# Half-width weight loads, longer filler bursts and a small fill moved from GpSimd to ScalarE, in an attention-and-mixer kernel on one Trainium2 core

## The chip, the cores and the metric

The kernel runs on one core of a Trainium2 chip. The metric is the device time of one execution in microseconds (us). "PE" is the matmul engine (TensorE), "PEld" its weight load, "ACT" ScalarE, "DVE" VectorE, "POOL" GpSimd, "SP" SyncE, which issues most of the DMAs. "L887" is line 887 of the kernel. The changed kernel is nine lines longer, so that L887 of the kernel before is L889 in the kernel after, L700 is L702, L453 is L454, L461 is L462 and L463 is L464.

## The reference

Two layers (the same weights twice), each an attention block and a token mixer. The sequence has S = 2048 tokens of D = 640 features; there are H = 32 heads of only 20 features each. A "chunk" below is a block of 128 x 512 scores, and the "crossing" is the way from the first layer to the second.

```python
def _A_ref(x, wqkv, wo):                       # attention
    qkv = (x @ wqkv).reshape(B, S, 3, H, Dh).transpose(2, 0, 3, 1, 4)
    q, k, v = qkv[0], qkv[1], qkv[2]
    p = _softmax(einsum("bhqd,bhkd->bhqk", q, k) * Dh ** -0.5)
    o = einsum("bhqk,bhkd->bhqd", p, v)
    return o.transpose(0, 2, 1, 3).reshape(B, S, D) @ wo
def _B_ref(x, w1, b1, w2, b2):                 # mixer over the tokens
    u = gelu(einsum("bsd,sf->bdf", layernorm(x), w1) + b1)
    return (einsum("bdf,fs->bds", u, w2) + b2).transpose(0, 2, 1)
x = A_x
for _ in range(2):                             # written out in the reference
    x = x + _A_ref(_layernorm(x), A_wqkv, A_wo)
    x = x + _B_ref(_layernorm(x), B_w1, B_b1, B_w2, B_b2)
```

One layer has 32 x 2048 x 2048 exponentials. They are the bulk of the work of ACT and DVE (L887 with 1520.2 of ACT's 1581.0 us busy, L840 and L860 with 507.4 and 636.4 of DVE's 1464.6, in the profile before); the score and P.V matmuls around them are the bulk of PE's (L700 and L927, with 575.2, 500.6 and 465.7 us, some of it at the same time, of 1646.1).

## The kernel before

The kernel is a Python program that plans its own order: a model of the engines (with constants such as `M_T`, `LAT_V`, `PAD_V`, `FILL_NS`) picks, one step at a time, what each engine does next, and emits the instruction. The order that comes out is fixed; each engine has its own list, with waits on semaphores where data are needed from another engine (section 1 shows a piece of ACT's list with its waits). Those waits are added by a tracker that compares which memory each instruction writes and reads.

The parts that matter here, with cuts marked `# ...`:

```python
PAD_V = 450.0
FILL_NS = 400.0                    # longest burst of filler matmuls, in ns of the model

# scores S: four 32-row tiles of the PE array side by side
pe(nc.tensor.matmul(dst, lhsT=k_, rhs=q_, start=True, stop=True, tile_position=(32 * j, 0)))      # L700
# their exponentials: most chunks by ACT ...
nc.scalar.activation(out=P[...], in_=St[...], func=ACT.Exp, scale=SCALE)                          # L887
# ... and some by DVE, with integer arithmetic (for a group of four chunks: L840 once for each chunk, then L860 five times)

# "filler" work of PE: projections, output projection, mixer, taken up between S and P.V
def do_fill(start, f, n):          # n is FILL_NS
    # ...
    while t - start < n:
        # ... stop before S would be late, or where the data are not there yet
        f["mms"][f["idx"]](f["tile"])
        t += f["cost"]
        # ...

# weights of Q (i = 1) and K (i = 0): one DMA into a staging tile, then five copies that spread
# the heads from 20 to 32 columns
def load_w(i):
    wr = sb("wraw", [128, NDT, D], BF16, i)
    # ...
    dma(wr[:], A_wqkv[:, coff:coff + D].rearrange("(dt p) n -> p dt n", p=128), 128 * NDT * D * 2,
        rate=DMA_RATE * (0.5 if i else 0.9), then=lambda t: pad_copies(i, wr, t))
def pad_copies(i, wr, t):
    wpad = wq_pad if i else wk_pad
    for dt_ in range(NDT):
        def f(s, eng, dt_=dt_):
            copy(eng, w_view(wpad, dt_)[:, :, 0:DH], wr[:, dt_, :].rearrange("p (h i) -> p h i", i=DH))
            # ...

# the constant columns of V: 20 values, then a one and three zeros, for each head and key tile
nc.scalar.activation(out=v_pad.bitcast(F32), in_=..., func=ACT.Copy, scale=0.0)
nc.scalar.activation(out=v_pad[:, :, 0:1], in_=..., func=ACT.Copy, scale=-2.0)                    # L1615
nc.gpsimd.memset(Vaug[:, NKT * H * VW:], 0.0)
nc.gpsimd.memset(Vv[:, :, H // 2, 0:32 - VW], 0.0)                                                # L1618
```

In the profile the staging tile appears as "JT" and the tile of V's weights as "attnT", because they share memory with those. `pst` is PSUM.

The softmax here doesn't subtract the row's maximum and nothing guards it: scores larger than these inputs give would overflow.

## Time and profile before

| | |
|---|---|
| time, first three runs | 1725.9 us, median of 3 (1723.1 to 1727.19) |
| time in the rounds of the kernel after (those three and one more) | 1726.55 us, median of 4 |
| time, in the five batches of experiments | 1724.36, 1724.84, 1724.95, 1724.72, 1724.65 us, medians of 9 to 11 |
| span of the profiled run, granted clock | 1722.5 us, 0.995 |

The page of the kernel before: first the busy time of each engine with its share of the span, then three groups of instructions (count, busy time and mean ns of one, idle time before them and its main releaser).

```profile
PE 1646.1 (96%) x21916; PEld 641.2 (37%) x21917; DVE 1464.6 (85%) x2630; ACT 1581.0 (92%) x1427; POOL 167.5 (10%) x261
...
L887 ACT ACTIVATE P<-pst 128x1536 bf16<-128x1536 f32 (+1 forms) x1335 | 1520.2, 1311 | 26.9 <-PE pst L700 14.5
L860 DVE TENSOR_SCALAR JT<-JT 128x2048 uint16<-128x2048 uint16 x950 | 636.4, 701 | 5.0 <-PE pst L927 1.8
L700 PE MATMUL pst<-QT,KT 32*128 32x512 bf16 (+1 forms) x4224 | 575.2, 377 | 40.7 <-ACT P L887 28.5
```

Busy time by stretches of the kernel before (start and end in us, length, then busy us of PE, PEld, DVE, ACT, POOL with their counts, the granted clock, the DMA share and GB/s).

```profile
0.00:20.00 20.00, 14.42 (x94) 6.23 (x98) 13.53 (x43) 12.45 (x16) 8.02 (x28) 0.83 0.67 221
20.00:40.00 20.00, 18.54 (x259) 7.16 (x253) 14.34 (x38) 19.45 (x20) 4.89 (x13) 1.00 0.12 35
...
100.00:400.00 300.00, 290.33 (x3580) 95.53 (x3580) 282.03 (x483) 294.78 (x262) 25.24 (x30) 1.00 0.03 8
...
780.00:1000.00 220.00, 210.17 (x3419) 110.81 (x3415) 118.70 (x248) 177.66 (x181) 22.36 (x49) 1.00 0.23 72
```

From 100 to 400 us ACT is busy 294.78 of 300 us and PE 290.33: these two engines leave little to win by a better order there. What is loose lies at the start and at the crossing between the layers (780 to 1000 us), where PE is full and ACT is not.

The timeline of the start, kernel before (start, length, engine, line, operation, count; in brackets the idle time just before it and what ended it):

```profile
7.84 0.20 POOL L1618 MEMSET Vaug<- 128x128 bf16 x1 [5.69 <-ACT Vaug L1615]
8.13 0.19 POOL L354 TENSOR_SCALAR rt<-mv 128x1 f32<-128x1 f32 x1
...
5.24 2.55 ACT L1615 ACTIVATE Vaug<-mhalf 128x512 bf16<-128x512 f32 x1
...
9.50 0.59 PE L541 MATMUL pst<-ident,attnT 128*128 128x128 bf16 x5 [3.30 <-DVE attnT L530]
...
13.71 3.03 PE L453 MATMUL pst<-hh,wq 128*128 128x512 bf16 x7 [0.24 <-DVE wq L463]
...
19.36 0.39 PE L700 MATMUL pst<-QT,KT 32*128 32x512 bf16 x3
```

POOL's tiny memset waits 5.69 us for ACT's fill of V's constant columns, and behind it in POOL's list stands the first step of the layernorm (`rt`), whose input was ready near 4.2 us. The way to the first score matmul at 19.36 us leads through it. PE is idle for 3.30 us before 9.50 us, and half clock follows (0.50 in the windows from 10 to 15 us). By the clock records of this trace it lasts 6.83 us, from 9.67 us on; the other windows of half clock within the span, in this trace, last 3.41 or 6.83 us. These records hold no granted clock but 1.00 and 0.50.

### The profile page before, as it was taken

What the parts mean: (1) busy time and instruction counts of PE and PEld (TensorE: products, weight loads), DVE (VectorE), ACT (ScalarE), POOL (GpSimd) and SP (SyncE); (2) the same over time, 40 slices, a digit from 0 to 9 for tenths busy, and PEclk for the clock granted to TensorE, in tenths of its full rate; (3) what the DMA queues carried; (4) which work ended last, traced back from release to release, by engine and by line L of the source; (5) the groups of instructions that cost most, each with busy time, mean ns of one, the idle gap of its engine ahead of it and who ended that gap; (6) DMA issues with size and microseconds to landing.
All of it is one profiled execution on the core that took longest, in us unless ns stands there. A gap on an engine that the chain in (4) does not pass through costs nothing. (4 is left out here: it accounts for less than half of the span.)

```text
span 1722.5 us, 50500 instructions
## 1 busy us (share of the span) xinstructions
PE 1646.1 (96%) x21916; PEld 641.2 (37%) x21917; DVE 1464.6 (85%) x2630; ACT 1581.0 (92%) x1427; POOL 167.5 (10%) x261
## 2 busy tenths in 40 slices
PE   8999999999999999998999999999999999998989
PEld 3433333332333333335545432333333333332356
DVE  6688999999989999999444489999999888999963
ACT  7899999999999999997598899999999999999950
POOL 3100002000200020001100000110011000200010
PEclk9999999999999999999999999999999999999999
DMA  3200001000112106511422000100002120257143
GB/s 119 29 2 2 2 13 36 2 1 2 52 57 71 39 32 190 182 34 43 148 84 75 25 2 2 33 32 1 1 17 58 57 70 32 76 179 216 42 125 95
DMA packets 103295, 98.06 MB, mean 57 GB/s; under 512 B 45600, under 2 KB 79520, under 8 KB 103072
## 3 DMA queue, kind: packets, MB, share of 16 engines
q1 hardware_dynamic: 99456, 94.82, 17.8%
q8 instruction: 171, 2.80, 0.7%
q0 software_dynamic: 3616, 0.01, 0.3%
q14 instruction: 52, 0.43, 0.1%
HBM read 63.35 MB, written 31.46 MB: 55 GB/s over the span
## 5 line engine op out<-in xcount | busy, mean ns | idle before, releaser
L887 ACT ACTIVATE P<-pst 128x1536 bf16<-128x1536 f32 (+1 forms) x1335 | 1520.2, 1311 | 26.9 <-PE pst L700 14.5
L860 DVE TENSOR_SCALAR JT<-JT 128x2048 uint16<-128x2048 uint16 x950 | 636.4, 701 | 5.0 <-PE pst L927 1.8
L700 PE MATMUL pst<-QT,KT 32*128 32x512 bf16 (+1 forms) x4224 | 575.2, 377 | 40.7 <-ACT P L887 28.5
L840 DVE TENSOR_SCALAR JT<-pst 128x512 uint16<-128x512 f32 x760 | 507.4, 679 | 63.9 <-PE pst L700 61.5
L927 PE MATMUL pst<-P,Vaug 128*32 128x512 bf16 (+1 forms) x3440 | 500.6, 380 | 3.4 <-DVE T_85 L977 1.8
L927 PE MATMUL pst<-JT,Vaug 128*32 128x512 bf16 (+1 forms) x3920 | 465.7, 380 | 3.4 <-DVE T_85 L977 2.4
L700 PEld LDWEIGHTS <-KT 32*128 32x128 bf16 x4224 | 168.5, 91 | 512.2 <-issue 498.5
L927 PEld LDWEIGHTS <-Vaug 128*32 128x32 bf16 x7360 | 170.2, 94 | 297.3 <-issue 268.0
L1002 POOL TENSOR_TENSOR T_86<-T_85,rden 128x512 bf16<-128x512 f32 x64 | 67.5, 1054 | 1130.6 <-DVE rden L989 1090.8
L1066 PE MATMUL pst<-wo,attnT 128*32 128x320 bf16 x2048 | 111.3, 301 | 4.7 <-DVE attnT L1012 3.2
L456 PEld LDWEIGHTS <-W 128*32 128x32 bf16 x3384 | 89.7, 96 | 60.0 <-issue 28.8
L1488 PE MATMUL pst<-ident,zw 128*32 128x512 bf16 (+1 forms) x330 | 108.8, 380 | 0.0
L456 PE MATMUL pst<-hh,wq 128*32 128x512 bf16 x1232 | 104.3, 382 | 1.3 <-DVE JT L840 0.7
L456 PE MATMUL pst<-hh,wk 128*32 128x512 bf16 x1240 | 97.3, 381 | 1.1 <-DVE JT L840 0.6
L456 PE MATMUL pst<-x1last,W 128*32 128x320 bf16 x1536 | 80.6, 301 | 0.9 <-DVE JT L840 0.5
L1066 PEld LDWEIGHTS <-attnT 128*32 128x32 bf16 x2048 | 52.4, 96 | 42.2 <-issue 20.3
L456 PE MATMUL pst<-attnT,hh 128*32 128x320 bf16 x1196 | 60.2, 300 | 2.1 <-DVE hh L463 0.7
L463 DVE CAST KT<-pst 128x512 bf16<-128x512 f32 x53 | 36.0, 680 | 19.5 <-PE pst L456 18.3
L456 PE MATMUL pst<-JT,W 128*32 128x320 bf16 x1080 | 52.3, 300 | 0.0
L977 DVE STREAM_TRANSPOSE T_85<-pst 128x512 f32<-128x512 f32 (+1 forms) x58 | 40.0, 690 | 8.1 <-PE pst L927 8.0
L354 POOL TENSOR_SCALAR rt<-mv 128x1 f32<-128x1 f32 x64 | 13.4, 209 | 340.2 <-DVE mv L346 339.6
L463 DVE CAST Vaug<-pst 128x320 bf16<-128x320 f32 x43 | 20.6, 482 | 30.4 <-PE pst L456 21.6
(91 smaller groups left out, 878.0 us busy)
## 6 DMA issues: line engine op xcount, KB each, us to landing
W<-in_B_w_dram SPq DMA_DIRECT2D x10, 768.0 KB
W<-in_B_w_dram SPq DMA_DIRECT2D x24, 256.0 KB
xs<-in_A_x_dram SPq DMA_DIRECT2D x32, 160.0 KB
x2d<-xs SPq DMA_DIRECT2D x16, 320.0 KB
xs<-x2d SPq DMA_DIRECT2D x16, 320.0 KB
x1d_69<-xs SPq DMA_DIRECT2D x12, 320.0 KB
uacca_72<-W SPq DMA_DIRECT2D x12, 320.0 KB
W<-uacca_72 SPq DMA_DIRECT2D x12, 320.0 KB
```

The source lines that it names most:

```text
L354: nc.gpsimd.tensor_scalar(out=rt[:], in0=mv[:, 1:2], scalar1=(1.0 + LN_EPS) if double else 1.0, scalar2=LN_EPS * LN_EPS if double else LN_ ...
L456: nc.tensor.matmul(out_[32 * c:32 * c + 32], lhsT=lhsT[:, 32 * c:32 * c + 32], rhs=rhs, start=start, stop=stop, tile_position=(0, 32 * c))
L463: nc.vector.tensor_copy(out=out_, in_=in_)
L700: pe(nc.tensor.matmul(dst, lhsT=k_, rhs=q_, start=True, stop=True, tile_position=(32 * j, 0)))
L840: nc.vector.tensor_scalar(out=c["jt"][:, j * 512:(j + 1) * 512], in0=Dt[:], scalar1=SCALE * LOG2E * 256.0, scalar2=127.0 * 256.0, op0=ALU. ...
L860: nc.vector.tensor_scalar(out=tt_[:], in0=c["jt"][:], scalar1=0.5, scalar2=TERM_C[i], op0=ALU.mult, op1=ALU.add)
L887: nc.scalar.activation(out=P[:, 0:n, :].rearrange("p a b -> p (a b)"), in_=St[:, 0:n, :].rearrange("p a b -> p (a b)"), func=ACT.Exp, scal ...
L927: pe(nc.tensor.matmul(dst, lhsT=Vaug[:, n:n + 32], rhs=ap, start=acc["cnt"][j] == 1 and not part, stop=last[j] and (half is None or part = ...
L977: nc.vector.transpose(out=T1[:], in_=src[:, 0:w])
L1002: eng.tensor_tensor(out=o_, in0=a_, in1=b_, op=ALU.mult)
L1066: nc.tensor.matmul(t[32 * c:32 * c + 32, 0:w], lhsT=q_, rhs=wo_pad[:, gg, c0:c1], start=(gi == 0), stop=(gi == len(gs) - 1), tile_position ...
L1488: pe(nc.tensor.matmul(dst[0:32, 0:128 * n], lhsT=zw[:, 0:32], rhs=ident[:].unsqueeze(1).to_broadcast([128, n, 128]), start=not inside, sto ...
```

## The change

Its intent: the weights of Q, K and V arrive in halves of the heads, so that the first projections (heads of the first half) can begin sooner; the zeros in V are written by ACT, so that POOL need not wait for ACT; and PE's filler matmuls come in longer bursts (`FILL_NS` 400 to 600), so that PE changes less often between row tiles (scores) and column tiles (everything else).

```diff
-PAD_V = 450.0
+PAD_V = 260.0
-FILL_NS = 400.0
+FILL_NS = 600.0
 # load_wv: V's weights by halves, the same pattern (cut)
-    def pad_copies(i, wr, t):
+    def pad_copies(i, hf, wr, t):
         # ... (w_left and w_time are kept by weight and half)
-                copy(eng, w_view(wpad, dt_)[:, :, 0:DH], wr[:, dt_, :].rearrange("p (h i) -> p h i", i=DH))
+                copy(eng, w_view(wpad, dt_)[:, h0:h1, 0:DH], wr[:, dt_, h0 * DH:h1 * DH].rearrange("p (h i) -> p h i", i=DH))
-            either.append((1.5, t, seq[0], PAD_V, 730.0, f))
+            either.append((1.5 if hf == 0 else 2.5, t, seq[0], PAD_V, 460.0, f))
-        def load_w(i):
+        def load_w(i, hf):
             wr = sb("wraw", [128, NDT, D], BF16, i)
+            c0, c1 = COLS[hf]
-            dma(wr[:], A_wqkv[:, coff:coff + D].rearrange("(dt p) n -> p dt n", p=128), 128 * NDT * D * 2,
-                rate=DMA_RATE * (0.5 if i else 0.9), then=lambda t: pad_copies(i, wr, t))
+            dma(wr[:, :, c0:c1], A_wqkv[:, coff + c0:coff + c1].rearrange("(dt p) n -> p dt n", p=128), 64 * NDT * D * 2,
+                rate=DMA_RATE * 0.5, prio=1 + hf, then=lambda t: pad_copies(i, hf, wr, t))
-        load_w(1)
-        load_w(0)
+        load_w(1, 0)
+        load_w(0, 0)
         # ... x tiles, load_wv(0), more x tiles
+        load_w(1, 1)
+        load_w(0, 1)
+        L0.load_wv(1)
-        nc.gpsimd.memset(Vv[:, :, H // 2, 0:32 - VW], 0.0)
+        nc.scalar.activation(out=Vv[:, :, H // 2, 0:32 - VW], in_=mhalf[...], func=ACT.Copy, scale=0.0)
```

More of the change, by code (lines that the diff above doesn't have):

```diff
@@ L255 @@
     n_warm = [0]
-    w_left = dict(Q=NDT, K=NDT)
-    w_time = dict(Q=0.0, K=0.0)
+    w_left = {(w, hf): NDT for w in "QK" for hf in range(2)}
+    w_time = {k: 0.0 for k in w_left}
     state = NS()
@@ L503, in new_layer @@
         L.wv = None
-        L.wv_ready = None
+        L.wv_ready = {}
         L.v_left = [NT, NT]
@@ L515, in make_producer, with load_wv @@
     def make_producer(L):
-        def load_wv():
+        def load_wv(hf):
             L.wv = sb("wv", [128, NDT, D], BF16)
-            dma(L.wv[:], A_wqkv[:, 2 * D:3 * D].rearrange("(dt p) n -> p dt n", p=128), 128 * NDT * D * 2,
-                then=lambda t: setattr(L, "wv_ready", t))
+            c0, c1 = COLS[hf]
+            dma(L.wv[:, :, c0:c1], A_wqkv[:, 2 * D + c0:2 * D + c1].rearrange("(dt p) n -> p dt n", p=128), 64 * NDT * D * 2,
+                prio=1 + hf, rate=DMA_RATE * 0.8, then=lambda t: L.wv_ready.update({hf: t}))
         def token_tile(tt, src, ready, release=None):
@@ L582, in evac @@
                         producer_done()
-                add_fill(mms, 136.0, evac, 400.0, ready=lambda: max(ready, L.wv_ready), pr=pr,
-                         urgent=lambda pr=pr: pr <= L.now_unit() + URG, acost=460.0, ok=lambda: L.wv_ready is not None)
+                add_fill(mms, 136.0, evac, 400.0, ready=lambda half=half: max(ready, L.wv_ready[half]), pr=pr,
+                         urgent=lambda pr=pr: pr <= L.now_unit() + URG, acost=460.0, ok=lambda half=half: half in L.wv_ready)
         def add_proj(what, g, b, ready):
@@ L620, in add_proj @@
                 pr = min(pr, L.need[("Q", 0, b)] + g)
-            add_fill(mms, PE_MM, evac, 600.0, ready=ready, pr=pr, ok=lambda: w_left[what] == 0 and (what == "K" or len(rQ) > 0),
-                     urgent=lambda: pr <= L.now_unit() + URG, acost=620.0, on_start=on_start, what=what)
+            add_fill(mms, PE_MM, evac, 600.0, ready=ready, pr=pr, ok=lambda: w_left[(what, g // 4)] == 0 and (what == "K" or len(rQ) > 0),
+                     urgent=lambda: pr <= L.now_unit() + URG, acost=620.0, on_start=on_start, what=(what, g // 4))
         def producer_done():
@@ L1416, in on_attnT_dead @@
             if L.nxt:
-                L.nxt.load_wv()
+                for hf in range(2):
+                    L.nxt.load_wv(hf)
         L.gelu_table = gelu_table
@@ L1565, in run_until @@
             best[1](best[0])
-    def pad_copies(i, wr, t):
+    def pad_copies(i, hf, wr, t):
         wpad = wq_pad if i else wk_pad
+        key = ("Q" if i else "K", hf)
+        h0, h1 = hf * H // 2, (hf + 1) * H // 2
         for dt_ in range(NDT):
             def f(s, eng, dt_=dt_):
-                copy(eng, w_view(wpad, dt_)[:, :, 0:DH], wr[:, dt_, :].rearrange("p (h i) -> p h i", i=DH))
-                w_left["Q" if i else "K"] -= 1
-                w_time["Q" if i else "K"] = max(w_time["Q" if i else "K"], s + (730 + LAT_ACT if eng == "ACT" else PAD_V + LAT_V))
+                copy(eng, w_view(wpad, dt_)[:, h0:h1, 0:DH], wr[:, dt_, h0 * DH:h1 * DH].rearrange("p (h i) -> p h i", i=DH))
+                w_left[key] -= 1
+                w_time[key] = max(w_time[key], s + (460 + LAT_ACT if eng == "ACT" else PAD_V + LAT_V))
             seq[0] += 1
-            either.append((1.5, t, seq[0], PAD_V, 730.0, f))
+            either.append((1.5 if hf == 0 else 2.5, t, seq[0], PAD_V, 460.0, f))
     def front(L0):
@@ L1584, in load_x0 @@
             rX0.want(f)
-        def load_w(i):
+        def load_w(i, hf):
             wr = sb("wraw", [128, NDT, D], BF16, i)
+            c0, c1 = COLS[hf]
             coff = 0 if i else D
-            dma(wr[:], A_wqkv[:, coff:coff + D].rearrange("(dt p) n -> p dt n", p=128), 128 * NDT * D * 2,
-                rate=DMA_RATE * (0.5 if i else 0.9), then=lambda t: pad_copies(i, wr, t))
+            dma(wr[:, :, c0:c1], A_wqkv[:, coff + c0:coff + c1].rearrange("(dt p) n -> p dt n", p=128), 64 * NDT * D * 2,
+                rate=DMA_RATE * 0.5, prio=1 + hf, then=lambda t: pad_copies(i, hf, wr, t))
         for tt in range(4):
             load_x0(tt)
-        load_w(1)
-        load_w(0)
+        load_w(1, 0)
+        load_w(0, 0)
         for tt in range(4, 6):
             load_x0(tt)
-        L0.load_wv()
+        L0.load_wv(0)
         for tt in range(6, NT):
             load_x0(tt)
+        load_w(1, 1)
+        load_w(0, 1)
+        L0.load_wv(1)
         nc.vector.memset(mhalf[:], -0.5)
@@ L1616, in front @@
         nc.gpsimd.memset(Vaug[:, NKT * H * VW:], 0.0)
-        nc.gpsimd.memset(Vv[:, :, H // 2, 0:32 - VW], 0.0)
+        nc.scalar.activation(out=Vv[:, :, H // 2, 0:32 - VW], in_=mhalf[:, 0:1].unsqueeze(2).to_broadcast([128, NKT, 32 - VW]), func=ACT.Copy, scale=0.0)
         clk.update(ACT=6000.0, DVE=1100.0, POOL=2200.0, PE=1300.0 + 427.0 * N_WARM0)
```

## The prediction

> **What bounds the kernel now.** Share of busy time (first part of the page): PE 96%, ACT 92%, DVE 85% of 1722.5 us. In the busy time by stretches, ACT is busy 98 to 99.8% and PE 95 to 99% nearly everywhere from 150 to 750 and from 1000 to 1600 us; DVE 90 to 99%. So the attention stages run at ACT and PE together. Exceptions: the start (0 to 100 us: ACT 85 us), the crossing between layers (780 to 1000 us: PE full, ACT short), and the tail.
>
> **The start, from the timeline.** POOL's second fill of Vaug waits 5.69 us for ACT's strided write (5.24 to 7.79 us). Behind it the first rt, whose mv was there at 4.17 us, starts only at 8.13. The fourth scaled tile comes at 11.72 us, the projections start at 13.71, the first S at 19.36, the first exp at 19.83, the second only at 23.30. PE has nothing between 6.20 and 9.50 us, and the granted clock is 0.50 from 10 to 16 us: the first 12 projection matmuls take about 4.2 us. [...]
>
> **What the change does** (order of instructions in both builds):
> - The zeros go to ACT, behind its other fills: POOL no longer waits, rt starts near 4.2 us.
> - Ten weight copies become twenty of half the size, 14 of them on ACT. Nine stand before ACT's first hh copy; at about 0.36 us each (estimate from 0.63 us between the starts of two 640-wide copies) they run from 8 to 11.3 us. The first projections need only half of the weights, so DMA should not hold them: before, about 1.5 MB had landed by 7 us (windows, GB/s).
> - I expect Q projections near 12 us, first S at 15.5 to 17.5, first exp near 17, and then six exps in a row instead of one exp and a gap. That is worth 3 to 5 us.
> - FILL_NS 600 makes bursts longer. Row/column changes on PE fall only from 2678 to 2638. One costs about 0.10 us (timeline at 40 us: S to PV 0.32 us for 0.22 us of streaming): about 3 to 4 us. Forty more column matmuls for P.V with JT, 8 fewer with P: +1.7 us.
> - The scheduler moves 8 chunks (4 in each layer) from ACT to DVE: 8 x 0.525 us = -4.2 us on ACT, two more groups of 4 x 679 + 5 x 701 ns = +12.4 us on DVE, which idles 258 us, mostly at the start and the crossing. The second layer hardly changes otherwise.
>
> **On the critical path:** the start (3 to 5 us), ACT's chunks (up to 4 us, if DVE has the slack), the changes of mode only where PE leads; they overlap. Sum about -8 us of 1726.
>
> **Prediction: 1717.5 us**, 8 in 10 between 1709 and 1725. Faster by over 2%: 0.02; within 2%: 0.96; slower by over 2%: 0.02.
>
> **Right or wrong:** POOL's wait for ACT gone; first S before 17.5 us; ACT busier from 16 to 40 us; crossing shifted earlier by 4 to 7 us, the second layer shorter by 1 to 3 us only; ACT's exp count 1331.
>
> **What would make it wrong:** half-width weight rows (640-byte pieces) landing so late that ACT's nine copies block its queue; long bursts delaying S so that ACT starves (exp waiting for PE, 14.5 us now, would grow); DVE becoming the last in the attention stages; the early gain given back at the crossing, where PE is full.

The sum stays at about -8 us of 1726, from 3 to 5 us for the start, up to 4 us for ACT's chunks and 3 to 4 us for the changes of mode, which overlap. Its figures for single steps are estimates from the profile before. A chunk's 0.525 us on ACT is from the mean exps of three chunks (128x1536, 1521 ns) and of two (128x1024, 1102 ns): (1521 + 1102) / 5. The +1.7 us comes out as 32 matmuls at a quarter of 0.22 us each, and about 0.22 us is what four more 512-column matmuls, one on each of four tiles, add to a run of them in the timeline (L456: runs of 4, 8 and 12 take 0.39, 0.60 and 0.82 us from 24 to 27 us). The 0.22 us "of streaming" is the same figure; section 3 works out the 0.10 us of a change.

## The result, and the profile after

In the same rounds the kernel before took 1726.55 us (median of 4 runs) and the kernel after 1731.76 us (median of 4, 1729.11 to 1733.35). The ratio is 1.0032, with a 95% interval from 1.0013 to 1.0051: within 2%, slower by a little, and 14 us above the predicted 1717.5. Here and below a ratio is the mean time of one kernel's runs over that of the other's of the same rounds, so it is not quite the ratio of the medians.

The page of the kernel after:

```profile
PE 1650.4 (95%) x21906; PEld 641.5 (37%) x21906; DVE 1477.9 (85%) x2650; ACT 1578.8 (91%) x1432; POOL 170.5 (10%) x260
...
L889 ACT ACTIVATE P<-pst 128x1536 bf16<-128x1536 f32 (+1 forms) x1331 | 1517.0, 1303 | 32.0 <-PE pst L702 18.8
L862 DVE TENSOR_SCALAR JT<-JT 128x2048 uint16<-128x2048 uint16 x960 | 648.0, 706 | 5.3 <-PE pst L929 2.3
L702 PE MATMUL pst<-QT,KT 32*128 32x512 bf16 (+1 forms) x4224 | 574.0, 377 | 41.5 <-ACT P L889 29.8
```

The shift of work came as predicted: 1335 to 1331 exp instructions, 3.2 us less busy time in them, and two more groups of five DVE instructions (950 to 960). But ACT now idles 32.0 us before its exps instead of 26.9, so it gave more back than it gained. By stretches:

```profile
0.00:20.00 20.00, 12.92 (x50) 5.58 (x51) 11.80 (x37) 12.49 (x21) 7.67 (x25) 0.83 0.76 221
20.00:40.00 20.00, 18.43 (x222) 6.56 (x220) 12.01 (x33) 17.45 (x21) 5.20 (x15) 1.00 0.09 27
...
100.00:400.00 300.00, 289.33 (x3572) 94.91 (x3571) 280.99 (x479) 294.98 (x263) 24.29 (x29) 1.00 0.03 8
...
780.00:1000.00 220.00, 209.60 (x3377) 111.50 (x3372) 117.15 (x245) 172.54 (x174) 21.80 (x49) 0.98 0.23 72
```

ACT has less work done in the first 40 us, not more (12.49 + 17.45 against 12.45 + 19.45), and the clock at the crossing is 0.98 instead of 1.00. The timeline of the start, kernel after:

```profile
4.33 0.19 POOL L355 TENSOR_SCALAR rt<-mv 128x1 f32<-128x1 f32 x1 [2.18 <-DVE mv L347]
...
8.04 0.44 ACT L462 COPY wq<-JT 128x320 bf16<-128x320 bf16 x1
13.23 1.54 ACT L462 COPY wq<-JT 128x320 bf16<-128x320 bf16 x4 [4.75 <-DMA JT<-in_A_wqkv_dram]
...
14.70 0.24 DVE L464 COPY wk<-JT 128x320 bf16<-128x320 bf16 x1 [4.90 <-DMA JT<-in_A_wqkv_dram]
...
10.81 2.74 PE L454 MATMUL pst<-attnT,hh 128*128 128x320 bf16 x10 [0.28 <-DMA attnT<-in_A_wqkv_dram]
16.84 2.29 PE L454 MATMUL pst<-hh,wq 128*128 128x512 bf16 x5 [3.29 <-ACT hh L462]
...
21.78 0.60 PE L702 MATMUL pst<-QT,KT 32*128 32x512 bf16 x5
```

POOL's wait is gone: `rt` starts at 4.33 us. But ACT makes one copy of Q's weights at 8.04 us and then stands still for 4.75 us until a DMA lands; DVE stands still 4.90 us in the same way; PE then waits 3.29 us for the copy of `hh` that stands behind those copies in ACT's list. The first score matmul comes at 21.78 us, 2.42 later than before.

I compared progress through the whole run: the start of the n-th score matmul in each trace. These are worked out from the trace; differences are against the kernel before. The two right columns are experiments, told of below.

| n-th score matmul (from 0) | before, us | after | split | zeros |
|---|---|---|---|---|
| 0 | 19.36 | +2.42 | -1.54 | -2.89 |
| 10 | 25.90 | +0.09 | -3.88 | -2.89 |
| 100 | 68.96 | +3.69 | -0.28 | -2.97 |
| 300 | 155.91 | +2.78 | -1.18 | -2.97 |
| 1200 | 481.13 | +3.32 | -0.61 | -2.96 |
| 2047 (end of attention 1) | 783.54 | +3.12 | +0.09 | -5.14 |
| 2176 (attention 2 begun) | 876.08 | +5.72 | -0.06 | -4.88 |
| 4223 (last) | 1646.53 | +6.49 | -0.85 | -4.65 |

So the kernel after lost some 3.7 us before 70 us, kept the loss to the end of the first attention, lost 2.6 us more at the crossing, and 0.8 us in the second layer.

### The profile page after: what moved, and what is told of

Its sections match the earlier page's. It is cut to its first block, busy times and chain, and to the rows that moved or that the text cites. A ratio compares the mean times of both kernels' runs of the same rounds, so it can differ in the third digit from the quotient of the medians.

```text
span 1730.2 us, 50511 instructions
## 1 busy us (share of the span) xinstructions
PE 1650.4 (95%) x21906; PEld 641.5 (37%) x21906; DVE 1477.9 (85%) x2650; ACT 1578.8 (91%) x1432; POOL 170.5 (10%) x260
## 5 line engine op out<-in xcount | busy, mean ns | idle before, releaser
L862 DVE TENSOR_SCALAR JT<-JT 128x2048 uint16<-128x2048 uint16 x960 | 648.0, 706 | 5.3 <-PE pst L929 2.3
L842 DVE TENSOR_SCALAR JT<-pst 128x512 uint16<-128x512 f32 x768 | 513.6, 680 | 55.0 <-PE pst L702 52.8
L702 PEld LDWEIGHTS <-KT 32*128 32x128 bf16 x4224 | 162.5, 91 | 506.6 <-issue 495.3
L457 PE MATMUL pst<-attnT,hh 128*32 128x320 bf16 x1140 | 56.0, 300 | 1.1 <-ACT hh L462 0.5
L464 DVE CAST QT<-pst 128x512 bf16<-128x512 f32 x59 | 39.7, 673 | 10.1 <-PE pst L457 9.8
```

Of the source, the lines that this page charges most:

```text
L457: nc.tensor.matmul(out_[32 * c:32 * c + 32], lhsT=lhsT[:, 32 * c:32 * c + 32], rhs=rhs, start=start, stop=stop, tile_position=(0, 32 * c))
L464: nc.vector.tensor_copy(out=out_, in_=in_)
L842: nc.vector.tensor_scalar(out=c["jt"][:, j * 512:(j + 1) * 512], in0=Dt[:], scalar1=SCALE * LOG2E * 256.0, scalar2=127.0 * 256.0, op0=ALU. ...
L862: nc.vector.tensor_scalar(out=tt_[:], in0=c["jt"][:], scalar1=0.5, scalar2=TERM_C[i], op0=ALU.mult, op1=ALU.add)
```

## The experiments

Eighteen runs were made, all correct. "Ratio" is to the kernel before in the same batch. I convert differences of ratios to us with 1725 us. "Half clock" is the mean over a kernel's runs of 2 x (1 - granted clock) x span, that is the us of half clock in it; the kernel before has 19.2 in its 51 runs.

| run | what | median us (range, runs) | ratio [95%] | half clock, us |
|---|---|---|---|---|
| split | after, halves stored apart | 1726.34 (1724.05-1728.31, 5) | 1.0010 [0.9997, 1.0022] | 21.4 |
| after_fill400 | after, FILL_NS 400 | 1732.48 (1731.71-1733.3, 5) | 1.0047 [1.0033, 1.0061] | 21.5 |
| split400 | split, FILL_NS 400 | 1724.68 (1722.29-1727.94, 5) | 1.0006 [0.9993, 1.0019] | 17.9 |
| zeros | before, zeros of V by ACT | 1721.30 (1720.0-1723.47, 5) | 0.9981 [0.9968, 0.9994] | 12.4 |
| fill600 | before, FILL_NS 600 | 1730.75 (1728.47-1732.29, 5) | 1.0034 [1.0021, 1.0047] | 34.6 |
| fill800 | before, FILL_NS 800 | 1728.85 (1723.95-1733.36, 6) | 1.0023 [1.0008, 1.0038] | 28.2 |
| zeros_fill600 | zeros, FILL_NS 600 | 1727.00 (1723.02-1730.67, 6) | 1.0015 [1.0001, 1.0028] | 24.7 |
| zeros_fill200 | zeros, FILL_NS 200 | 1732.96 (1730.47-1733.53, 5) | 1.0044 [1.0032, 1.0056] | 23.5 |
| zeros_warm | zeros, 230 dummy matmuls | 1724.43 (1723.01-1729.08, 5) | 1.0005 [0.9993, 1.0017] | 7.6 |
| zeros_late | zeros, 72 late dummies | 1722.83 (1721.79-1725.76, 5) | 0.9992 [0.998, 1.0004] | 11.0 |
| fill600_late | fill600, 77 late dummies | 1728.06 (1727.14-1732.27, 5) | 1.0024 [1.0012, 1.0036] | 22.1 |
| jitter_mt | zeros, M_T 410 | 1723.06 (1719.87-1723.51, 5) | 0.9983 [0.997, 0.9995] | 23.4 |
| jitter_lat | zeros, LAT_V 121 | 1723.72 (1720.78-1725.27, 5) | 0.9988 [0.9975, 1.0001] | 22.7 |
| jitter_sd | zeros, SD_WAIT 510 | 1725.57 (1723.98-1726.61, 5) | 1.0001 [0.9987, 1.0015] | 24.8 |
| jitter_mp | zeros, M_P 160 | 1722.83 (1720.74-1725.03, 5) | 0.9986 [0.9973, 0.9998] | 17.9 |
| f600_mt | zeros_fill600, M_T 410 | 1723.12 (1722.5-1726.82, 5) | 0.9993 [0.9982, 1.0005] | 22.0 |
| f600_mp | zeros_fill600, M_P 160 | 1727.78 (1724.32-1731.15, 6) | 1.0014 [1.0, 1.0028] | 25.9 |

The eighteenth, fill600_warm, is fill600 without timed rounds (below).

### 1. The wait at the start: split, after_fill400, split400

Theory: the second copy on ACT needs only the first half of Q's weights, which had landed at 6.74 us by the trace's landing times, but it waits for the DMA of the *second* half, which landed at 13.21 us (the copy started at 13.23). DVE's copy of K's weights waits in the same way for the second half of K, landed at 14.67 (it started at 14.70; the first half had landed at 8.71). The waits stand in the program itself. ACT's list in the kernel after and in split, with the semaphores that each instruction waits for (not a profile; `DMAHW4` is the queue of Q's first half, `DMAHW3` of Q's second, `DMAHW5` and `DMAHW4` of K's first and second):

```
after:  wq<-JT 128x16x20 [waits DMAHW4]      split:  wq<-JT 128x16x20 [waits DMAHW4]
        wq<-JT 128x16x20 [waits DMAHW3]              wq<-JT 128x16x20 x4
        wq<-JT 128x16x20 x3                          wk<-JT 128x16x20 [waits DMAHW5]
        wk<-JT 128x16x20 [waits DMAHW5]              wk<-JT 128x16x20 x3
        wk<-JT 128x16x20 [waits DMAHW4]              ...
        wk<-JT 128x16x20 x2                          wq<-JT 128x16x20 [waits DMAHW3]
```

No byte that the second copy reads is written by that DMA. But the second half is written with a stride: 320 columns from column 320 of each of five rows. From its first to its last byte it covers rows 1 to 4 whole. My reading is that the tracker compares such ranges and finds row 1 inside; row 0's first half lies before the range, and indeed only row 0's copy does not wait. The test: store the halves apart, so that neither range touches the other, and change nothing else.

```diff
-            wr = sb("wraw", [128, NDT, D], BF16, i)
+            wr = sb("wraw", [128, 2, NDT, D // 2], BF16, i)[:, hf]
-            dma(wr[:, :, c0:c1], A_wqkv[...], ...)
+            dma(wr[:], A_wqkv[...], ...)
-                copy(eng, ..., wr[:, dt_, h0 * DH:h1 * DH].rearrange(...))
+                copy(eng, ..., wr[:, dt_, :].rearrange(...))
```

The order of the instructions is the same as in the kernel after on all five engines; only waits differ.

> The changed kernel with the two weight halves laid out one after the other in the staging tile instead of side by side in each row; the order of instructions is the same on every engine, only the wait of the copies for the DMA of the other half is gone. Theory A (the copies of the first half wait for the second half, and that is most of the loss): ACT's second wq copy starts right after its first (about 8.4 us instead of 13.23), the first S comes at 16.5 to 18 us instead of 21.8, and the kernel gains 3 to 5 us on the changed one: ratio to before 0.999 to 1.001. Theory B (the loss is in the rescheduled attention stages and the longer bursts): the start is as early, but less than 2 us of it reaches the end: ratio to before 1.002 or more.

The timeline of the start of split:

```profile
8.03 1.88 ACT L462 COPY wq<-JT 128x320 bf16<-128x320 bf16 x5
9.82 1.53 ACT L462 COPY wk<-JT 128x320 bf16<-128x320 bf16 x4
...
18.26 6.88 ACT L889 ACTIVATE P<-pst 128x1536 bf16<-128x1536 f32 x6 [0.45 <-PE pst L702]
...
10.49 2.83 PE L454 MATMUL pst<-attnT,hh 128*128 128x320 bf16 x10
13.11 2.34 PE L454 MATMUL pst<-hh,wq 128*128 128x512 bf16 x5
...
17.82 0.60 PE L702 MATMUL pst<-QT,KT 32*128 32x512 bf16 x5
...
28.00 0.60 PE L702 MATMUL pst<-QT,KT 32*128 32x512 bf16 x5
```

The nine copies run without a gap from 8.03 to 11.3 us, as the prediction had them. The first score matmul comes at 17.82 us, 3.96 us earlier than in the kernel after. That lead holds to the 100th score matmul (+3.69 against -0.28, a difference of 3.97) and to the 1200th (3.93). The time falls from a ratio of 1.0032 to 1.0010, 3.8 us; the runs of the two kernels do not overlap (1729.11 to 1733.35 and 1724.05 to 1728.31 us), though the two intervals together leave some 4 us of doubt, up or down, on the size. (In these two traces the lead grows to 7.34 us at the last score matmul; split was profiled at a clock of 0.996, the kernel after at 0.991, so I take the timed runs for the worth.) So the false wait is shown, and it is paid at the end as well.

The same pair with the old burst length:

```diff
-FILL_NS = 600.0
+FILL_NS = 400.0
```

> The changed kernel with FILL_NS back at 400. Theory A: still late at the start (first S near 21.8 us, copies waiting until 13.2 us) and slower than before: ratio 1.001 to 1.004. Theory B: the loss is gone: ratio 0.998 to 1.000.

> The changed kernel with the halves stored apart (no wait for the other half) and FILL_NS 400: the weights by halves and the zeros on ACT, without the longer bursts. Theory A (the wait for the other half is what the halves cost): about 4 us less than after_fill400 (1732.5 us), so 1727 to 1729 us, and the first S near 17.8 us as in split. If the halves were good once freed of the wait, it should reach the 1721.3 us of zeros or less; I expect it does not, because the first S of split (17.82 us) is later than that of zeros (16.47 us).

Ratios 1.0047 and 1.0006, and a first score matmul at 15.30 us in split400 (I had expected a gain of 4 us and 17.8 us): here the wait costs 7.1 us, clear of the intervals. It is a loss of the change in both settings. That after_fill400 is no faster than the kernel after was against my idea, at that time, that FILL_NS 600 was the main cost.

split400 shows something more. Its first score matmul comes 4.06 us earlier than in the kernel before, and number 10 comes 6.40 earlier. By number 20 the lead is 3.00, by the hundredth 1.02, by the 150th it is 0.55 *behind*. The last 1.57 us of this go between the 100th and the 110th, and there the trace has a window of half clock (70.36 to 73.77 us); after_fill400, with the same order and no such window there, loses 0.04 us from the 100th to the 150th. For the rest, the profile shows where ACT stood still. What ACT waited for from 20 to 100 us (total, times, longest), first split400, then zeros, which started 1.17 us later:

```profile
ACT P L889 <- PE pst L702: 5.4, 7, 1.5
ACT KT L462 <- PE pst L457: 3.3, 2, 2.0
ACT Vaug L462 <- PE pst L457: 2.3, 3, 1.1
```

```profile
ACT KT L461 <- PE pst L456: 2.4, 2, 1.3
ACT P L887 <- PE pst L700: 1.7, 4, 0.6
ACT Vaug L461 <- PE pst L456: 1.5, 2, 1.1
ACT P L887 <- PE pst L927: 1.3, 2, 0.8
```

ACT waits for PE 11.0 us in split400 and 6.9 us in zeros. As I read it, early exps need keys and values that PE has not projected yet, and exps that start early only wait later. In split, too, six exps in a row start at 18.26 us, and the next score matmul after 22.93 us comes only at 28.00. So I take PE's filler work, and not the first exp, for the limit of the first 100 us. That the halves are worth nothing for this reason is my reading of these waits; it is not separated from that window of half clock, nor from the luck of the order that section 5 measures.

### 2. The zeros of V alone: zeros

```diff
-        nc.gpsimd.memset(Vv[:, :, H // 2, 0:32 - VW], 0.0)
+        nc.scalar.activation(out=Vv[:, :, H // 2, 0:32 - VW], in_=mhalf[...], func=ACT.Copy, scale=0.0)
```

> The kernel before with the zeros in V moved to ACT alone; all other engines keep their order. Theory A: POOL's 5.7 us wait is gone, the fourth scaled tile comes near 8.5 us instead of 11.72, the first projection near 11 to 12 us instead of 13.7 (the weights land at 9.1 and 11.4 us), first S near 17 us, and 2 us (ratio 0.9985 to 0.9995) reach the end. Theory B: the start is earlier but nothing reaches the end: ratio 1.000.

Everything else in the lists of all five engines stays in the same order. The timeline of zeros:

```profile
4.36 0.19 POOL L354 TENSOR_SCALAR rt<-mv 128x1 f32<-128x1 f32 x1 [2.21 <-DVE mv L346]
...
10.71 2.04 PE L453 MATMUL pst<-hh,wq 128*128 128x512 bf16 x7 [0.48 <-ACT hh L461]
...
16.47 0.39 PE L700 MATMUL pst<-QT,KT 32*128 32x512 bf16 x3
```

The first score matmul comes 2.89 us earlier, and the shift stays between 2.89 and 3.26 us up to the 1200th; the median is 3.1 us lower, the ratio 0.9981 (3.3 us). This one line is the gain of the change, and the version beats both kernels. The wait that it removes was itself of the kind of section 1: the memset writes columns 0 to 7 of one head's 24, ACT's fill the columns 20 to 23 of every head, and no byte is common.

### 3. The burst length alone: fill600, fill800, zeros_fill600, zeros_fill200

```diff
-FILL_NS = 400.0
+FILL_NS = 600.0     (fill800: 800.0; zeros_fill200: 200.0)
```

> The kernel before with FILL_NS 600 alone. Theory A: the longer bursts do nothing much, ratio 0.999 to 1.001, the first S unchanged at 19.4 us. Theory B: the longer bursts cost what the change lost: ratio 1.002 to 1.004, with more time of ACT waiting for S.

> The kernel before with FILL_NS 800 (bursts up to four full or six narrow matmuls). Theory C (bursts concentrate the filling work and leave PE with sparse stretches): mean granted clock at or below 0.991 and a ratio of 1.003 to 1.006. Rival D (the loss with 600 is luck of one reshuffled schedule): any ratio between 0.998 and 1.003, not tied to the clock.

> The kernel before with the zeros on ACT and FILL_NS 600, without the halves. If the parts add: 1721.3 + 5.8 = 1727 us, ratio 1.0010 to 1.0020. Then the halves, freed of the wait (split, 1726.3 us), cost nothing at FILL_NS 600. If the start sets it, as the progress in the traces suggests, it should instead lie 2 to 4 us under split: 1722 to 1724 us.

> The kernel before with the zeros on ACT and shorter bursts than before: one full or two narrow matmuls. Theory C, if it holds in both directions: at most 12 us of half clock and 1718 to 1722 us. If mode changes between bursts cost more than the evenness gains, slower than zeros by 1 to 4 us, with more changes of mode on PE. If the order of the work is a lottery (rival D), anything within 1718 to 1730.

fill600 costs 5.9 us against before (1.0034), and zeros_fill600 the same against zeros (1.0015 against 0.9981). (The moved zeros are worth 3.3 us here too: 1.0034 against 1.0015.) fill600's page:

```profile
L887 ACT ACTIVATE P<-pst 128x1536 bf16<-128x1536 f32 (+1 forms) x1331 | 1516.9, 1305 | 34.8 <-PE pst L700 20.9
L860 DVE TENSOR_SCALAR JT<-JT 128x2048 uint16<-128x2048 uint16 x960 | 646.6, 704 | 5.2 <-PE pst L927 2.2
```

The whole shift of chunks from ACT to DVE, which I had counted as up to 4 us of gain, is in this run (1331 exps, 960 DVE instructions), and the run is slower: ACT saves 3.3 us of busy time and idles 7.9 us more before its exps. Most of that is exps that wait for their score matmuls (20.9 us against 14.5 in the kernel before), a risk that the prediction had listed. In both traces of fill600 (the second is fill600_warm) the 2176th score matmul is level with the kernel before (-0.08 and +0.21 us) and the last one late by 3.44 and 5.60 us: the time is lost in the second layer. The changes of PE between row and column tiles fell by about 40 of 2,700 in the program order, and no gain is to be seen. The trace shows what a change goes with: in the kernel before, three score matmuls start at 40.49 us and the P.V matmuls after them at 40.81, 0.32 us later; four of these P.V matmuls, of the same width, are followed by column-tile matmuls, without a change, after 0.23 us (41.04). Over the whole trace, where PE had not waited, the medians are 0.322 us in 484 places of the first kind and 0.226 us in 216 of the second (worked out from the starts), so I estimate about 0.10 us for a change. But 40 such changes less in a span where PE is not alone the limit did not show in the time.

200, 400, 600 and 800 ns gave 1732.96 (with zeros), 1721.30 (with zeros) or 1724.4 (without), 1730.75 and 1728.85 us: no trend. The outer two missed what theory C, which blames the clock, had expected of them: fill800 lost less than fill600 (1.0023), and zeros_fill200 was 10.9 us slower than zeros. 400 is a sharp best. A constant that had been tuned together with the rest would look like this. That led to two more questions: is it the clock, and is it luck?

### 4. The clock: fill600_warm, zeros_warm, zeros_late, fill600_late

fill600 has most half clock of all (34.6 us against 19.2). In the kernel after, such windows lie at the crossing. Four stretches of 3.4 us of the kernel after around it (columns as above; the granted clock is the third number from the end):

```profile
788.20:791.60 3.40, 2.09 (x38) 0.96 (x31) 3.39 (x7) 3.40 (x4) 0.00 (x0) 1.00 0.34 99
791.60:795.00 3.40, 2.90 (x44) 1.35 (x43) 3.01 (x7) 2.81 (x3) 0.61 (x1) 0.50 0.02 5
...
801.80:805.20 3.40, 0.97 (x23) 0.37 (x12) 3.23 (x10) 2.03 (x3) 1.95 (x5) 1.00 0.00 0
805.20:808.60 3.40, 3.26 (x33) 1.65 (x34) 2.69 (x8) 0.00 (x0) 2.04 (x5) 0.50 0.07 11
```

Here a stretch in which PE is busy 2.09 or 0.97 of 3.40 us is followed by one of half clock. That share alone does not decide it: in the kernel before PE is busy 1.82 of 3.40 us from 798.20 us and 1.65 from 801.60 us, and the clock stays 1.00 in both and in the stretch after them. What decides it these runs do not show; theory C, that sparse stretches of PE bring the half clock, is a guess under test. The experiments put dummy matmuls (zero weights, added into an open sum) into gaps that the model foresees:

```diff
+        if o[0] > now + 250 and sum(h[1] for h in hist) < 12.0 and now > 20000 and a.want and not a.done and a.acc_open():
+            return (o[0], lambda s, n=min(4, int((o[0] - now) / PE_MM + 0.3)), o=o: keep_warm(s, n, o[3]))
+    def keep_warm(start, k, then):                    # k dummies, then the step that was due
+        ...
+            nc.tensor.matmul(a.acc["tile"][0:32, 0:128 * n], lhsT=zw[:, 0:32], rhs=ident[...], start=False, stop=False, tile_position=(0, 0))
+        then(start)
 # zeros_late, fill600_late: only from unit 380 of 512 on (a.now_unit() >= 380 in place of now > 20000)
```

> Placeholder look at fill600 again with a profile: theory C (the longer bursts leave stretches of PE with little work, and PE's granted clock then falls to half) expects some 20 to 35 us at half clock again, in other places of the span or the same; a rival (chance placement of the clock) expects about 15 us as in before.

The kernel was fill600 itself, without the dummies, so the expectation does not apply. It repeats: 1730.87 us, clock 0.991.

> The kernel zeros with 230 extra dummy matmuls in gaps that the schedule expects on PE; nothing else in another place. Theory C: half clock after 20 us falls from about 7 to 10 us to under 4 us, and the time falls by 1 to 4 us, to 1717 to 1720 us. If the dummies stand in PE's way rather than in its gaps, it gets slower by up to 50 us divided by the share that hits, at most some 10 us.

> zeros (1721.3 us) with the same kind of 72 late dummies. Theory C: a small gain, 0 to 2 us, as zeros has only 12 us at half clock in the mean; rival: slower by the dummies' own time, up to 72 x 0.22 = 16 us if none falls in a gap, and 1 to 3 us if most do.

> This is the run that was meant as fill600_warm, which by mistake was sent as the unchanged fill600. It is fill600 (1730.8 us) with 77 extra dummy matmuls on PE in gaps that the schedule expects late in each layer's attention, where its half-clock windows lay (787, 1463, 1544, 1654 us); every other instruction keeps its place. Theory C (the longer bursts lose time through the clock): half clock in the mean of the runs falls from 35 us to under 18 us and the time falls by 3 to 6 us, to 1725 to 1728 us. Rival D (the clock is a side effect, the loss is in the order of the work): half clock falls, the time by less than 2 us.

zeros_warm kept the clock (half clock 7.6 us instead of 12.4; the profiled run has none) and was 4 us slower than zeros: 230 dummies cost more than the clock returns. zeros_late changed little (11.0 us of half clock, 1.9 us slower, within the intervals). fill600_late brought half clock down from 34.6 to 22.1 us and 1.7 us back (1.0034 to 1.0024), which is within the intervals too. Within each kernel, over all 144 timed runs here, a run with 1 us more half clock took about 0.19 us longer (a regression, so an estimate, not an experiment). At that rate the 15.4 us more of half clock in fill600 are worth 2.9 of its 5.9 us. So the clock may be a part of it, but not the whole. By the same estimate the 8 to 35 us of half clock of the kernels in the table are worth some 1 to 7 us of about 1725. (The 0.22 us for each dummy in the expectation of zeros_late is an estimate too, from the runs of 512-column matmuls named beside the prediction.)

### 5. Luck of the order: jitter_mt, jitter_lat, jitter_sd, jitter_mp, f600_mt, f600_mp

Rival: a changed constant reorders PE's list (a large part of PE's list stands in another order in fill600), and any such order is a draw. Four constants of the model that say nothing of bursts or of the start were moved by 1 to 7%, on top of zeros, one in each run:

```diff
-M_T = 400.0        -LAT_V = 120.0        -SD_WAIT = 500.0        -M_P = 150.0
+M_T = 410.0        +LAT_V = 121.0        +SD_WAIT = 510.0        +M_P = 160.0
```

> zeros with one constant of the scheduler's model moved from 400 to 410 ns; bursts, work and start unchanged, thousands of instructions reordered. Theory 'the length of the bursts costs the 5.8 us': within 1.5 us of zeros, that is ratio 0.997 to 0.999. Rival 'any reordering is a draw that scatters the time by several us': the four jitter runs spread over 3 us or more, mostly above zeros, ratios between 0.998 and 1.004.

> zeros with the modelled latency of V's path 121 instead of 120 ns; again only an order. Burst theory: ratio 0.997 to 0.999. Draw theory: anywhere from 0.998 to 1.004.

> zeros with a threshold of the scheduler at 510 instead of 500 ns; only an order. Burst theory: ratio 0.997 to 0.999. Draw theory: anywhere from 0.998 to 1.004.

> zeros with a constant of the scheduler at 160 instead of 150 ns; the least reordered of the four. Burst theory: ratio 0.997 to 0.999. Draw theory: anywhere from 0.998 to 1.004, and nearer to zeros than the other three, since it is reordered least.

Ratios 0.9983, 0.9988, 1.0001, 0.9986, with zeros itself at 0.9981. (jitter_mp reorders PE's list least, jitter_mt most.) The work is the same, 1335 exps, but for jitter_mt with 1337. So the five orders spread over 0.0020, or 3.5 us; three lie within 1.3 us of zeros, as the burst theory said, and one outside. Two such ratios have some 3 us of doubt between them, so only jitter_sd differs from zeros by more than the noise, and just so. The mean of the five is 0.9988, and the best is zeros itself, that is the order of the kernel before. In their profiled runs, jitter_lat, jitter_sd and jitter_mp lose 3.0 to 3.9 us against zeros between score matmuls 2100 and 2150 at the crossing; jitter_sd's granted clock from 800 to 830 us is 0.95, where zeros and jitter_mt have 1.00; single traces, so only a hint of where.

Then two of the same moves on top of zeros_fill600:

```diff
 FILL_NS = 600.0
-M_T = 400.0        -M_P = 150.0
+M_T = 410.0        +M_P = 160.0
```

> zeros and FILL_NS 600, with the model's constant of 400 ns at 410. Theory 'FILL_NS 600 costs time in this kernel, whatever the order': ratio 1.001 or more, like zeros_fill600 (1.0015) and about 5 us above the five orders with FILL_NS 400 (mean 0.9988). Rival 'zeros_fill600 was a bad draw': ratio between 0.998 and 1.000.

> zeros and FILL_NS 600, with the constant of 150 ns at 160, which here changes only about 160 lines of PE's order, in the second half of the run. Theory 'FILL_NS 600 costs time whatever the order': ratio 1.001 or more. Rival 'bad draw': mostly the same order as zeros_fill600, so also near 1.0015 unless the few places changed are those that cost; it tells little by itself and is here as the measure of how far two almost equal orders lie apart.

f600_mp, whose order differs from zeros_fill600 in only 159 lines of PE's listing, repeats it: 1.0014 against 1.0015. f600_mt, another order altogether, is at 0.9993, 3.8 us faster at the same burst length, and inside the spread of the orders with 400. It is not quite the same work: it moved half of the chunks only (1333 exps, against 1331 in zeros_fill600 and 1335 in zeros). So the 5.9 us of fill600 and zeros_fill600 are not what bursts of 600 cost in every order. Pair by pair, 600 against 400 cost 5.9 us (before), 5.9 (zeros), 1.7 (jitter_mt), 4.8 (jitter_mp), 0.7 (split) and gave 2.6 (after), each with 3 to 4 us of doubt. Before and zeros have one order, the orders of zeros_fill600 and f600_mp are nearly one, and split has that of after, so these six pairs are about three independent draws. In all six pairs ACT idles more before its exps with 600, by 7.9, 8.3, 6.6, 9.4, 2.5 and 1.8 us in the same sequence, while the exps themselves take 2.4 to 3.3 us less: the larger the wait, the larger, in the main, the cost. These are single traces, and fill800 does not fit (25.8 us idle before exps, 1.0023), so it is a hint and no proof. Whether long bursts cost a little over many orders stays open; in none of the six pairs was the predicted gain of 3 to 4 us measured.

## Why the prediction was wrong, point by point

Along one path from before to after, the measured steps are: zeros to ACT -3.3 us; FILL_NS 600 on top (zeros_fill600) +5.9; the weights by halves without the false wait (split) -0.9, within the noise; the false wait (after) +3.8. They add up to the +5.5 of the result because each is a difference to the step before, and another path gives other middle steps: with bursts of 400 the halves cost 4.3 us (split400 against zeros) and the false wait 7.1. The first step is the same 3.3 us with both burst lengths, and the last one is a loss with both.

- **"POOL no longer waits, rt starts near 4.2 us": right.** 4.33 us after, 4.36 in zeros. The predicted 3 to 5 us for the start is what this step alone gives, at its low end: 3.3 us.
- **"The first projections need only half of the weights, so DMA should not hold them": this step failed.** The first half had landed at 6.74 us, but the second copy was made to wait for the second half until 13.21 us. I had looked at bytes and bandwidth, and not at which DMA each copy waits for, although the listing of the program with its waits shows it without any run. The prediction had listed late rows blocking ACT's queue as a risk; the queue was blocked, but the rows that it needed were not late. The narrow rows themselves cost little: the pieces have 640 bytes, and the windows of split show 350 GB/s from 7 to 10 us and 335 from 10 to 15, against 364 and 354 before with 1280-byte rows, that is 4 to 5% less in stretches that hold other transfers too.
- **First score matmul at 15.5 to 17.5 us, ACT busier from 16 to 40 us: wrong** for the kernel after (21.78 us; ACT 17.45 us busy from 20 to 40 against 19.45). Split, without the false wait, came to 17.82.
- **"Six exps in a row instead of one exp and a gap": right in form** (six from 22.22 us on in the kernel after), and worth nothing at the end: in split400 a lead of 6.40 us was spent by the 150th score matmul, with ACT waiting for PE and one window of half clock.
- **FILL_NS 600 "about 3 to 4 us" by fewer changes of mode: failed.** The changes fell as counted; fill600 was 5.9 us slower, and its exps waited 20.9 us for score matmuls instead of 14.5. The term was an estimate of a cost on PE that was taken as time of the kernel. How much of the loss is the long bursts and how much the order they drew stays open.
- **"Up to 4 us" from eight chunks moved from ACT to DVE: failed as a gain.** The chunks moved (1335 to 1331 exps, 3.2 us less exp time), and ACT idled 5.1 us more before its exps.
- **"The crossing shifted earlier by 4 to 7 us, the second layer shorter by 1 to 3 us": wrong.** It came 3.12 us later, lost 2.6 us in the crossing and 0.8 us after.
- **The range:** 1709 to 1725 us counted gains, each argued from one engine, and left no room for what any new order does. Five orders of all but the same work spread over 3.5 us, some of it noise.

Settled: the false wait, the worth of the moved zeros, and that the longer bursts brought none of their predicted gain to the kernel before. Open: the exact cause in each bad order (about half of fill600's loss goes with half clock by a regression), and whether the halves, with the false wait removed, would gain in a well-tuned order.

## What to carry to other kernels

When one tile is loaded in pieces, store each piece as one unbroken range of its own, and read the listing of waits of the first consumers before believing that a piece can be used early; two such false waits sat at the start of these kernels, 5.69 us in the one and 4.75 us in the other. Judge a change of a planned order against the spread of a few harmless reorderings of the same kernel, not against the one tuned order alone. And time won for an engine that waits for another one later is not won: follow the progress of one instruction through the whole run to see whether a lead lasts.
